# Retention and mixture of experts on one core: zero products in the first gaps, masks made on the chip, and routing steps written later in the program

## The chip, the cores and the metric

The kernel runs on one core of a Trainium2 chip. TensorE (PE in the rows) multiplies, with weight loads shown as PEld; VectorE is DVE, ScalarE is ACT, GpSimd is POOL, and SyncE is SP, which here issues nearly all loads. The metric is device microseconds for one execution of the whole program; less is better.

## The reference

```python
for t in range(S):                                   # B=4, H=8, S=768, D=64
    state = gamma * state + einsum('bhd,bhe->bhde', k[:, :, t], v[:, :, t])
    y[:, :, t] = scale * einsum('bhd,bhde->bhe', q[:, :, t], state)
x = y.transpose(0, 2, 1, 3).reshape(3072, 512)
logits = x @ w_gate + modality_bias[modality_id]     # 8 experts
e_idx = argmax(logits); gate_w = softmax(logits) at e_idx
out[mask_e] = gate_w * (relu(x[mask_e] @ w1[e]) @ w2[e])   # w1 512x1024, w2 1024x512
```

So: a retention (linear attention with a decay per head) over 3072 tokens, then each token goes through the one expert of the eight that its logits choose.

## The kernel before, in words

**Retention.** The 3072 tokens are 24 chunks of 128, six to a batch row. For chunk n PE makes the scores `sc` (line 174), whose product with a triangular mask DVE writes to `abuf` (line 179); the products `y` of the query with the state `s` of the chunk before (line 198) and of `abuf` with the decayed values `vd` (line 210); the state `st` (line 246), which ACT copies to `s` (line 251); and the tokens `x` (line 227), which are `yT` times a matrix of an identity and the gate weights, and which ACT copies to `xs` (line 231). DVE makes `yT` out of `y` (line 217) and sums the logits `lg` (line 232); POOL makes `vd` (line 162); ACT makes the table `dq` (line 156). Chunks 0 and 1 run singly (`one_chunk`), the others in pairs (`two_chunks`); in the pair n, n+1 the scores are those of chunks n+2 and n+3 and the tokens those of n-2 and n-1.

**Routing.** After every six chunks the group of six is routed. `route_a` finds the expert (parts 0 and 1) and the gate value (part 2: `den`, `rec`); `route_b` counts ranks on PE (`rk`, lines 369 and 370); `route_c` turns them into row numbers (`rkt`, `pos`). `scatter` then has POOL write the group's chunks, one by one, to `xsl`, a buffer in device memory sorted by expert (line 391). There are nine `xs` tiles, so the copy of chunk 9 into its tile first waits until the scatter of chunk 0 has landed.

**Experts.** Jobs of 512 slots each run behind the retention: two early ones (`e0`, `e1`), placed when twelve chunks are routed, and four at the end (`f0` to `f3`). A job loads its rows (`rows_in`: `xb`), transposes them on DVE (line 710), splits them into a high and a low part (ACT line 716, DVE line 725: `xT`), does the same with its weights (`raw`, `cut`), and multiplies (line 733: `h`; line 751: `o`), 32 steps of six products each. The results are scaled by the gate (lines 763 to 766) and scattered to the output by POOL (line 767).

**What sets the order.** PE, ACT, DVE and SP take their instructions in the order in which the program writes them. The pairs have named places ("top", "st", "sc", "pr", "tk", "end"), and `at(n, place, f)` hangs a routing or job step on the place of chunk n. All small PE results share eight banks of PSUM through the one tag "bank"; a tile waits until the bank's last reader is through. `warm` multiplies zeros, with no use for the result, before the first scores and after them.

Of the kernel before, what the change touches and what calls it, by code (L numbers as in the profile page):

```python
# [46 lines left out]
WARM = (10, 4)  # L47
# [8 lines left out]
def kernel(  # L56
# [199 lines left out]
    def warm(i):  # L256

        z = abuf[:, 3, 0, : DM // 2]
        if i == 0:
            nc.vector.memset(z, 0.0)  # L260
        z = z.bitcast(BF16)
        w = bank("warm")
        for _ in range(WARM[i]):
            nc.tensor.matmul(w, z[:, :P], z, start=True, stop=True)

    gates = cp.tile([P, NG, NE], F32, name="gates")

# [476 lines left out]
    def second(s, hh, part):  # L746
# [9 lines left out]
        if part == 3:  # L756
# [4 lines left out]
            if s is jobs[-1] and hh == HH - 1:  # L761
                h = DM // 2
                nc.vector.tensor_scalar(o[:, h:], s.po[:, h:], gate, None, op0=ALU.mult)
                nc.scalar.activation(o[:, :h], s.po[:, :h], AF.Copy, scale=gate)
            else:
                nc.scalar.activation(o, s.po, AF.Copy, scale=gate)  # L766
# [127 lines left out]
    for g in range(NGRP - 1):  # L894
# [3 lines left out]
        at(t + 2, "st", route_b, g)  # L898
        early = g + 1 in EARLY
        if early:  # L900
            at(t + 2, "st", early_a, g + 1)
        at(t + 2, "st", route_c, g)
        at(t + 2, "st", route_a, g, 2)
# [11 lines left out]
        places = [(2, "end"), (3, "sc"), (4, "sc"), (4, "end"), (6, "sc"), (6, "end")]  # L915
        if early or t + 6 == NN:
            places[2:] = [(4, "sc"), (4, "end"), (5, "sc"), (5, "end")]
# [6 lines left out]
    at(t + 3, "sc", two, raw, e, 1, (2, 3))  # L924
    at(t + 6, "top", rows_in, e)
    at(t + 6, "sc", cut, e, 1, 0, True)
    at(t + 6, "end", raw, e, 2, 0)
    n = t + 8
    at(n, "sc", flip_t, e, 0)
    at(n, "sc", flip_hi, e, 0)  # L930
    at(n, "tk", flip_lo, e, 0)
# [10 lines left out]
    def loads(n):  # L942

        for i in (n, n + 1):
            if i < NN:
                load_kq(i)
        for i in (n, n + 1):
            if i < NN:
                load_kv(i)

# [43 lines left out]
    def one_chunk(n):  # L994
# [3 lines left out]
        state(n)  # L998
        decay_q(n)
# [9 lines left out]
        heads_a(n)  # L1009
        run(n, "end")  # L1010
# [10 lines left out]
    def last_tokens():  # L1021
        g = NGRP - 1
        tokens_out(NN - 1)
        assert not hooks, hooks
        yield
# [86 lines left out]
    with tc.manual_schedule(engines={PE, ACT, DVE, SP}):  # L1112
        load_kq(0, True)
        nc.scalar.dma_start(cst, consts[:, :C_BIG])
        nc.scalar.dma_start(csq, consts[:, C_BIG:])
# [3 lines left out]
        nc.sync.dma_start(dcq, decq)  # L1119
        load_kv(1)  # L1120
        for n in range(SINGLE, LEAD, 2):
            loads(n)
# [9 lines left out]
        warm(0)  # L1132
        scores(0)
# [6 lines left out]
        tokens_out(NN - 2)  # L1140
# [28 lines left out]
def _layout(inputs):  # L1169
# [14 lines left out]
    cst = np.zeros((P, C_BIG + C_END), f)  # L1184
# [81 lines left out]
```

## Time and profile before

| | |
|---|---|
| time, median of 3 runs | 391.02 us (390.77 to 391.48) |
| the profiled execution's own time | 388.42 us |
| its span, first to last instruction | 386.6 us |
| TensorE busy | 374.3 us, 97% |
| VectorE, ScalarE, GpSimd busy | 203.7, 156.1, 100.6 us |
| HBM read and written | 65.05 and 23.41 MB |

The profiled execution is 2.6 us shorter than the median; sums are made on the profiled one and carried over as a difference. A row of the timeline gives start, duration, engine, line, operation, out<-in, count, and in brackets how long the engine stood idle and what released it. A busy PE may still be waiting inside a group of products; such a wait shows as a longer group.

### The profile page before, as it was taken

To read this page: it belongs to the slowest core of one execution; us is meant where nothing else is said; L and a number is where in the kernel's file an instruction comes from. 1 tells how busy PE (TensorE), PEld (TensorE's weight loads), DVE (VectorE), ACT (ScalarE), POOL (GpSimd) and SP (SyncE) were. 2 spreads that over 40 slices of the span, in tenths; PEclk is the share of its full clock that TensorE was granted. 3 is DMA by queue.
4 is the path that set the end of the run, shared out by engine and by line. 5 is a ranking of instruction groups with operands and counts; after the bars stand their busy time and mean duration, and the time that the engine had idled before them with its cause. 6 is when DMAs were issued, how large, how long until landed. Compare 5 with 4: busy or idle time off the path is not lost. (4 is left out here: it accounts for less than half of the span.)

```text
span 386.6 us, 7963 instructions
## 1 busy us (share of the span) xinstructions
PE 374.3 (97%) x2977; PEld 311.1 (80%) x2977; DVE 203.7 (53%) x418; ACT 156.1 (40%) x303; POOL 100.6 (26%) x141
## 2 busy tenths in 40 slices
PE   8999999999899999999999999999999999999993
PEld 4799888987787788888877888778888888888882
DVE  1876858868668982448243382433832466144100
ACT  1455535553665262345423453224532344244110
POOL 1342474664810887100210102101021002100121
PEclk9999999999999999999999999999999999999998
DMA  7999899999449659497973878738343674400001
GB/s 266 390 376 391 345 332 382 317 412 200 162 125 231 242 200 323 173 191 267 326 278 98 182 249 316 280 112 165 108 163 110 160 166 152 148 28 3 27 27 52
DMA packets 40474, 81.94 MB, mean 212 GB/s; under 512 B 8173, under 2 KB 20589, under 8 KB 40177
## 3 DMA queue, kind: packets, MB, share of 16 engines
q1 hardware_dynamic: 34720, 65.72, 54.1%
q0 software_dynamic: 5136, 15.21, 10.1%
q8 instruction: 25, 0.41, 0.4%
q10 hardware_dynamic: 576, 0.46, 0.4%
q14 instruction: 17, 0.14, 0.1%
HBM read 65.05 MB, written 23.41 MB: 229 GB/s over the span
## 5 line engine op out<-in xcount | busy, mean ns | idle before, releaser
L733 PE MATMUL h_f<-xT_f,hi_f 128*128 128x512 f32 x256 | 81.1, 392 | 0.0
L751 PE MATMUL o_f<-hi_f,hT_f 128*128 128x512 f32 x256 | 78.8, 389 | 0.0
L696 DVE TENSOR_TENSOR lo_f<-raw_f,hi_f 128x1024 fp32r<-128x1024 f32 x32 | 39.2, 1226 | 34.0 <-ACT hi_f L691 33.8
L733 PEld LDWEIGHTS h_f<-xT_f,hi_f 128*128 128x128 f32 x256 | 48.1, 188 | 11.1 <-issue 1.2
L751 PEld LDWEIGHTS o_f<-hi_f,hT_f 128*128 128x128 f32 x256 | 48.1, 188 | 10.0
L741 DVE SCALAR_TENSOR_TENSOR hT_f<-h_f,hT_f 128x512 fp32r<-128x512 f32 x32 | 22.2, 693 | 63.2 <-ACT hT_f L740 63.2
L733 PE MATMUL h_f<-xT_f,lo_f 128*128 128x512 f32 x128 | 49.9, 390 | 0.0
L751 PE MATMUL o_f<-lo_f,hT_f 128*128 128x512 f32 x128 | 49.8, 389 | 0.0
L767 POOL DMA_INDIRECT out_dram<-o_f,tg_f x16 | 15.7, 982 | 127.1 <-ACT o_f L766 112.3
L740 ACT ACTIVATE hT_f<-h_f 128x512 fp32r<-128x512 f32 x32 | 19.2, 599 | 54.4 <-PE h_f L733 54.4
L733 PE MATMUL h_e<-xT_e,hi_e 128*128 128x512 f32 x128 | 40.6, 393 | 0.0
L751 PE MATMUL o_e<-hi_e,hT_e 128*128 128x512 f32 x128 | 39.5, 390 | 0.0
L179 DVE TENSOR_TENSOR abuf<-sc,csq 128x512 f32<-128x512 f32 x48 | 30.1, 680 | 13.8 <-PE sc L174 7.1
L691 ACT CAST hi_f<-raw_f 128x1024 fp32r<-128x1024 f32 x32 | 33.3, 1041 | 0.0
L162 POOL TENSOR_TENSOR vd<-kv,cst 128x512 f32<-128x512 f32 x24 | 24.9, 1044 | 31.7 <-DMA kv<-in_qkv_dram 16.6
L751 PEld LDWEIGHTS o_f<-lo_f,hT_f 128*128 128x128 f32 x128 | 24.0, 188 | 5.0
L733 PEld LDWEIGHTS h_e<-xT_e,hi_e 128*128 128x128 f32 x128 | 24.0, 188 | 4.9
L751 PEld LDWEIGHTS o_e<-hi_e,hT_e 128*128 128x128 f32 x128 | 23.9, 188 | 4.9
L733 PEld LDWEIGHTS h_f<-xT_f,lo_f 128*128 128x128 f32 x128 | 24.0, 188 | 4.8
L766 ACT ACTIVATE o_f<-o_f,tg_f 128x512 f32<-128x512 f32 x15 | 10.3, 689 | 42.7 <-PE o_f L751 42.7
L174 PE MATMUL sc<-kq 64*128 64x128 f32 x384 | 27.0, 282 | 0.5 <-DMA kq<-in_qkv_dram 0.3
L391 POOL DMA_INDIRECT xsl<-xs,pos x24 | 25.4, 1059 | 7.7 <-POOL xs L387 5.3
(168 smaller groups left out, 526.3 us busy)
## 6 DMA issues: line engine op xcount, KB each, us to landing
raw_f<-in_w_dram SPq DMA_DIRECT2D x32, 512.0 KB, 3.5
kq<-in_qkv_dram SPq DMA_DIRECT2D x23, 512.0 KB, 7.0
kv<-in_qkv_dram SPq DMA_DIRECT2D x19, 512.0 KB, 9.1
raw_e<-in_w_dram SPq DMA_DIRECT2D x16, 512.0 KB, 4.3
xb_f<-xsl SPq DMA_DIRECT2D x16, 256.0 KB, 5.8
abuf<-in_w_dram SPq DMA_DIRECT2D x8, 512.0 KB, 4.8
rw<-in_w_dram SPq DMA_DIRECT2D x16, 256.0 KB, 6.8
xb_e<-xsl SPq DMA_DIRECT2D x8, 256.0 KB, 6.0
```

The source lines that it names most:

```text
L162: nc.gpsimd.tensor_tensor(vds[n], vv, dec[:, n % NCH].unsqueeze(2).to_broadcast([P, H, D]), op=ALU.mult)
L174: nc.tensor.matmul(pe[j][:, g * P : (g + 1) * P], kt[r, g], qt[r, g], start=True, stop=True, skip_group_check=True,)
L179: nc.vector.tensor_tensor(a[:, j], pe[j].rearrange("p (h t) -> p h t", t=P), mask.unsqueeze(1).to_broadcast([P, NG, P]), op=ALU.mult,)
L391: ins = nc.gpsimd.indirect_dma_start(out=xsl[:, :], out_offset=bass.IndirectOffsetOnAxis(ap=mid[gr][:, i : i + 1], axis=0), in_=xs.rearran ...
L691: nc.scalar.copy(hi, t)
L696: nc.vector.tensor_tensor(lo, t, hi.bitcast(F32), op=ALU.subtract)
L733: nc.tensor.matmul(s.ph, s.w[1][f // 2][wi][:, o : o + P], s.xT[kc][a], start=(kc == 0 and k == 0), stop=(kc == KC - 1 and k == 2),)
L740: nc.scalar.activation(hi, s.ph, AF.Relu)
L741: nc.vector.scalar_tensor_tensor(lo, s.ph, 0.0, hi.bitcast(F32), op0=ALU.max, op1=ALU.subtract)
L751: nc.tensor.matmul(s.po, s.hT[f][a][:, hh * P : (hh + 1) * P], s.w[2][f // 2][wi][:, (f % 2) * DM : (f % 2 + 1) * DM], start=(f == 0 and k ...
L766: nc.scalar.activation(o, s.po, AF.Copy, scale=gate)
L767: ins = nc.gpsimd.indirect_dma_start(out=out[:, :], out_offset=bass.IndirectOffsetOnAxis(ap=s.tg.bitcast(I32)[:, hh, 0:1], axis=0), in_=o, ...
```

## The change

It consists of these parts.

- `warm`: 12 instead of 10 zero products before the first scores, 4 after them as before, and new ones in chunk 0: 2 behind its state and 3 behind its `y`.
- The identity and the triangular mask (`csq`) are no longer loaded (128 KB on ACT's queue). POOL makes a ramp by an iota, and DVE compares it twice.
- The table `dcq` (256 KB), asked for ahead of the keys and values of chunk 1 before, is asked for behind the third load of keys and queries.
- In the groups that are not early, `route_b` moves from "st" to "tk" of the second pair, and `route_c` and the gate value to its "end"; the first two scatters move half a chunk or so.
- The first job's transposes (`flip_t`, `flip_hi`, `flip_lo` for its first quarter) move from "sc" and "tk" of chunk 20 to "top" and "sc" of chunk 21. Two of its weight loads move behind `rows_in`.
- The tokens of chunks 22 and 23 are written one step of the first job later.
- The last result is halved between DVE and ACT by partitions (64 x 512 each) instead of by columns (128 x 256 each), and the two are declared independent.

```diff
-WARM = (10, 4)
+WARM = (12, 4, 2, 3)
...
+    def setup_masks():
+        pin(
+            nc.gpsimd.iota(
+                ident, [[1, P]], base=0, channel_multiplier=-1,
+                allow_small_or_imprecise_dtypes=True,
+            )
+        )
+        nc.vector.tensor_scalar(mask, ident, 0.0, None, op0=ALU.is_ge)
+        nc.vector.tensor_scalar(ident, ident, 0.0, None, op0=ALU.is_equal)
...
-                h = DM // 2
-                nc.vector.tensor_scalar(o[:, h:], s.po[:, h:], gate, None, op0=ALU.mult)
-                nc.scalar.activation(o[:, :h], s.po[:, :h], AF.Copy, scale=gate)
+                a, b = slice(0, D), slice(D, P)
+                ins = nc.vector.tensor_scalar(o[a], s.po[a], gate[a], None, op0=ALU.mult)
+                disjoint(ins, "halves")
+                ins = nc.scalar.activation(o[b], s.po[b], AF.Copy, scale=gate[b])
+                disjoint(ins, "halves")
...
-        at(t + 2, "st", route_b, g)
         early = g + 1 in EARLY
+        at(t + 2, "st" if early else "tk", route_b, g)
...
-        at(t + 2, "st", route_c, g)
-        at(t + 2, "st", route_a, g, 2)
+        at(t + 2, "st" if early else "end", route_c, g)
+        at(t + 2, "st" if early else "end", route_a, g, 2)
...
-        places = [(2, "end"), (3, "sc"), (4, "sc"), (4, "end"), (6, "sc"), (6, "end")]
-        if early or t + 6 == NN:
-            places[2:] = [(4, "sc"), (4, "end"), (5, "sc"), (5, "end")]
+        places = [(3, "sc"), (3, "end"), (4, "sc"), (4, "end"), (6, "sc"), (6, "end")]
+        if t + 6 == NN:
+            places[4:] = [(5, "sc"), (5, "end")]
+        if early:
+            places = [(2, "end"), (3, "sc"), (4, "sc"), (4, "end"), (5, "sc"), (5, "end")]
...
-    at(t + 3, "sc", two, raw, e, 1, (2, 3))
     at(t + 6, "top", rows_in, e)
+    at(t + 6, "top", two, raw, e, 1, (2, 3))
...
-    at(n, "sc", flip_t, e, 0)
-    at(n, "sc", flip_hi, e, 0)
-    at(n, "tk", flip_lo, e, 0)
+    at(n + 1, "top", flip_t, e, 0)
+    at(n + 1, "top", flip_hi, e, 0)
+    at(n + 1, "sc", flip_lo, e, 0)
...
         state(n)
+        if n == 0:
+            warm(2)
...
         heads_a(n)
+        if n == 0:
+            warm(3)
...
         g = NGRP - 1
+        tokens_out(NN - 2)
+        yield
         tokens_out(NN - 1)
         assert not hooks, hooks
-        yield
         yield
...
-        nc.scalar.dma_start(cst, consts[:, :C_BIG])
-        nc.scalar.dma_start(csq, consts[:, C_BIG:])
+        nc.scalar.dma_start(cst, consts)
...
-        nc.sync.dma_start(dcq, decq)
```

**The order on DVE, around the scores of chunks 10 and 11.** These are DVE's instructions from `yT` of chunk 7 on, before and then in the change; the number behind a name is the program's own counter, and `abuf<-sc_10` is the masking of the scores of chunk 10.

```order
L217 TENSOR_TENSOR yT_710<-y_7_661,dq_587 128x256
L179 TENSOR_TENSOR abuf<-sc_10_738,csq 128x512
L179 TENSOR_TENSOR abuf<-sc_10_739,csq 128x512
L376 TENSOR_TENSOR rkt_753<-rk_750,oh_652 128x48
L379 TENSOR_REDUCE pos_755<-rkt_753 128x6
L361 TENSOR_REDUCE den_757<-ex_91 128x6
L363 RECIPROCAL rec_759<-den_757 128x6
L179 TENSOR_TENSOR abuf<-sc_11_761,csq 128x512
L179 TENSOR_TENSOR abuf<-sc_11_762,csq 128x512
L232 TENSOR_REDUCE lg_775<-xs_776 128x8
L232 TENSOR_REDUCE lg_775<-xs_786 128x8
```

```order
L217 TENSOR_TENSOR yT_721<-y_7_672,dq_598 128x256
L179 TENSOR_TENSOR abuf<-sc_10_749,csq 128x512
L179 TENSOR_TENSOR abuf<-sc_10_750,csq 128x512
L179 TENSOR_TENSOR abuf<-sc_11_761,csq 128x512
L179 TENSOR_TENSOR abuf<-sc_11_762,csq 128x512
L232 TENSOR_REDUCE lg_775<-xs_776 128x8
L232 TENSOR_REDUCE lg_775<-xs_789 128x8
L377 TENSOR_TENSOR rkt_804<-rk_786,oh_663 128x48
L380 TENSOR_REDUCE pos_806<-rkt_804 128x6
L362 TENSOR_REDUCE den_808<-ex_91 128x6
L364 RECIPROCAL rec_810<-den_808 128x6
```

The four routing instructions, of which `pos` and `rec` are what the scatters wait for, stand behind the masking of chunk 11 and the logits of chunks 6 and 7. At chunks 22 and 23 the same four move in the same way.

**The order on DVE, around chunks 22 and 23.** These rows follow the masking of chunk 22; `x_e` is the first job's first transpose, which needs the rows `xb_e`, and `xT_e<-x_e,xT_e` is its low part. ACT makes the high part (line 716) out of the same transpose; that cast stands, before, in front of ACT's four copies `xs` of chunks 18 and 19, and in the change behind them and behind the table `dq`.

```order
L376 TENSOR_TENSOR rkt_1665<-rk_1662,oh_1579 128x48
L379 TENSOR_REDUCE pos_1667<-rkt_1665 128x6
L361 TENSOR_REDUCE den_1669<-ex_91 128x6
L363 RECIPROCAL rec_1671<-den_1669 128x6
L179 TENSOR_TENSOR abuf<-sc_23_1673,csq 128x512
L179 TENSOR_TENSOR abuf<-sc_23_1674,csq 128x512
L710 STREAM_TRANSPOSE x_e_1687<-xb_e_1501 128x512
L232 TENSOR_REDUCE lg_1691<-xs_1692 128x8
L725 TENSOR_TENSOR xT_e_1689<-x_e_1687,xT_e_1689 128x512
L232 TENSOR_REDUCE lg_1691<-xs_1703 128x8
L217 TENSOR_TENSOR yT_1751<-y_20_1723,dq_1565 128x256
```

```order
L232 TENSOR_REDUCE lg_1687<-xs_1688 128x8
L232 TENSOR_REDUCE lg_1687<-xs_1701 128x8
L377 TENSOR_TENSOR rkt_1716<-rk_1698,oh_1590 128x48
L380 TENSOR_REDUCE pos_1718<-rkt_1716 128x6
L362 TENSOR_REDUCE den_1720<-ex_91 128x6
L364 RECIPROCAL rec_1722<-den_1720 128x6
L711 STREAM_TRANSPOSE x_e_1724<-xb_e_1508 128x512
L217 TENSOR_TENSOR yT_1756<-y_20_1728,dq_1576 128x256
L217 TENSOR_TENSOR yT_1756<-y_20_1729,dq_1576 128x256
L726 TENSOR_TENSOR xT_e_1726<-x_e_1724,xT_e_1726 128x512
```

The logits of chunks 18 and 19 no longer stand behind the transpose, and the low part stands behind `yT` of chunk 20. The transpose itself stays ahead of `yT` of chunk 20.

**The order on PE, where the first job begins.** The first row of each is the last of the retention's `y`; `x_0` and `x_1` are the two halves of a chunk's tokens, first those of chunk 22 and then those of chunk 23, and `h_e` are the first job's products.

```order
L210 MATMUL y_23_1838<-abuf,vd_1685 64x128 x4
L227 MATMUL x_0_1881<-wgt,yT_1855 128x136 x2
L227 MATMUL x_1_1885<-wgt,yT_1855 128x136 x2
L733 MATMUL h_e_1896<-xT_e_1689,hi_e_1541 128x512
L733 MATMUL h_e_1896<-xT_e_1689,lo_e_1543 128x512
L733 MATMUL h_e_1896<-xT_e_1689,hi_e_1541 128x512
L733 MATMUL h_e_1896<-xT_e_1781,hi_e_1541 128x512
L733 MATMUL h_e_1896<-xT_e_1781,lo_e_1543 128x512
L733 MATMUL h_e_1896<-xT_e_1781,hi_e_1541 128x512
L227 MATMUL x_0_1904<-wgt,yT_1872 128x136 x2
```

```order
L210 MATMUL y_23_1849<-abuf,vd_1685 64x128 x4
L734 MATMUL h_e_1897<-xT_e_1726,hi_e_1552 128x512
L734 MATMUL h_e_1897<-xT_e_1726,lo_e_1554 128x512
L734 MATMUL h_e_1897<-xT_e_1726,hi_e_1552 128x512
L734 MATMUL h_e_1897<-xT_e_1792,hi_e_1552 128x512
L734 MATMUL h_e_1897<-xT_e_1792,lo_e_1554 128x512
L734 MATMUL h_e_1897<-xT_e_1792,hi_e_1552 128x512
L227 MATMUL x_0_1905<-wgt,yT_1866 128x136 x2
L227 MATMUL x_1_1909<-wgt,yT_1866 128x136 x2
```

The job's first step of six products now stands ahead of the tokens of chunk 22, and its second step ahead of those of chunk 23.

## Rows read from the trace of the kernel before

**Rows 1.** The page's first part: busy time, share of the span, instructions.

```profile
PE 374.3 (97%) x2977; PEld 311.1 (80%) x2977; DVE 203.7 (53%) x418; ACT 156.1 (40%) x303; POOL 100.6 (26%) x141
```

**Rows 2.** Windows: stretch, length, busy of PE, PEld, DVE, ACT, POOL, clock, DMA, GB/s.

```profile
5.00:10.00 5.00, 4.68 (x60) 3.08 (x60) 1.47 (x3) 0.37 (x1) 1.04 (x1) 1.00 1.04 392
...
90.00:100.00 10.00, 8.08 (x118) 6.90 (x120) 7.70 (x23) 4.13 (x14) 4.59 (x10) 1.00 0.87 189
```

**Rows 3.** Timeline of the opening.

```profile
1.19 4.45 PE L264 MATMUL warm<-abuf 128*128 128x512 bf16 x10 [1.19 <-DVE abuf L260]
...
6.38 1.04 POOL L162 TENSOR_TENSOR vd<-kv,cst 128x512 f32<-128x512 f32 x1 [5.38 <-DMA cst<-in_consts_dram]
...
6.66 1.04 PE L264 MATMUL warm<-abuf 128*128 128x512 bf16 x4
...
7.85 1.29 DVE L179 TENSOR_TENSOR abuf<-sc,csq 128x512 f32<-128x512 f32 x2 [6.71 <-DMA csq<-in_consts_dram]
...
8.63 1.16 PE L174 MATMUL sc<-kq 64*128 64x128 f32 x16 [0.32 <-DMA kq<-in_qkv_dram]
...
10.63 1.04 POOL L162 TENSOR_TENSOR vd<-kv,cst 128x512 f32<-128x512 f32 x1 [3.21 <-DMA kv<-in_qkv_dram]
...
11.73 0.69 PE L246 MATMUL st<-vd,kv 128*64 128x64 f32 x16 [0.91 <-POOL vd L162]
```

**Rows 4.** Timeline around the first group's gate values and its first scatter.

```profile
44.66 0.19 DVE L363 RECIPROCAL rec<-den 128x6 f32<-128x6 f32 x1
44.77 1.25 DVE L179 TENSOR_TENSOR abuf<-sc,csq 128x512 f32<-128x512 f32 x2
...
45.93 0.32 DVE L232 TENSOR_REDUCE lg<-xs 128x8 f32<-128x32 f32 x2
46.02 1.18 POOL L391 DMA_INDIRECT xsl<-xs,pos  x1 [0.76 <-ACT xs L231]
...
55.33 0.67 ACT L231 COPY xs<-x 128x272 f32<-128x272 f32 x2 [2.86 <-DMA xsl<-xs,pos]
...
56.38 0.87 PE L246 MATMUL st<-vd,kv 128*64 128x64 f32 x16
```

**Rows 5.** DMA issued from 47.5 to 48.0: KB each, us to landing.

```profile
kv<-in_qkv_dram SPq DMA_DIRECT2D x1, 256.0 KB, 11.3
xsl<-xs,pos POOLq DMA_INDIRECT x1, 8.9
```

**Rows 6.** Timeline from the scores of chunk 23 to the first job.

```profile
91.95 1.49 PE L174 MATMUL sc<-kq 64*128 64x128 f32 x16
...
96.67 0.71 DVE L710 STREAM_TRANSPOSE x_e<-xb_e 128x512 f32<-128x512 f32 x1 [0.67 <-DMA xb_e<-xsl]
...
97.42 0.62 ACT L716 CAST xT_e<-x_e 128x512 fp32r<-128x512 f32 x1 [5.12 <-DVE x_e L710]
97.94 1.24 ACT L231 COPY xs<-x 128x272 f32<-128x272 f32 x4
...
98.38 0.66 PE L198 MATMUL y<-kq,s 64*64 64x128 f32 x14 [1.88 <-ACT xs L231]
...
98.77 0.69 DVE L725 TENSOR_TENSOR xT_e<-x_e,xT_e 128x512 fp32r<-128x512 f32 x1
...
101.01 0.86 DVE L217 TENSOR_TENSOR yT<-y,dq 128x256 f32<-128x256 f32 x2 [0.48 <-PE y L210]
...
104.42 1.97 PE L210 MATMUL y<-abuf,vd 128*64 128x128 f32 x32
...
107.03 1.16 PE L227 MATMUL x<-wgt,yT 128*128 128x136 f32 x8 [0.65 <-DVE yT L217]
...
109.43 1.09 PE L227 MATMUL x<-wgt,yT 128*128 128x136 f32 x8
```

**Rows 7.** Timeline of the last result.

```profile
380.17 0.48 DVE L763 TENSOR_SCALAR o_f<-o_f,tg_f 128x256 f32<-128x256 f32 x1 [20.37 <-PE o_f L751]
380.69 0.47 ACT L764 ACTIVATE o_f<-o_f,tg_f 128x256 f32<-128x256 f32 x1 [5.27 <-DVE o_f L763]
```

More of the change, by code (lines that the diff above doesn't have):

```diff
@@ L254, in small @@
         return cp.tile(shape, dt, name=nm)
[L256 to L264, printed above, removed]
-    gates = cp.tile([P, NG, NE], F32, name="gates")
+    gates = cp.tile([P, NG, NE], F32, name="gates")
+    def setup_masks():
[7 more added lines that the diff above has]
+        nc.vector.tensor_scalar(ident, ident, 0.0, None, op0=ALU.is_equal)
     def setup_a():
@@ L940, with loads @@
     at(n + 3, "sc", flip_lo, e, 3)
-    def loads(n):
+    def loads(n, tab=None):
         for i in (n, n + 1):
@@ L946, in loads @@
                 load_kq(i)
+                if tab is not None and i == n:
+                    nc.sync.dma_start(tab, decq)
         for i in (n, n + 1):
@@ L949, in loads, with warm @@
                 load_kv(i)
+    def warm(i):
+        z = abuf[:, 3, 0, : DM // 2]
+        if i == 0:
+            nc.vector.memset(z, 0.0)
+        z = z.bitcast(BF16)
+        w = bank("warm")
+        for _ in range(WARM[i]):
+            nc.tensor.matmul(w, z[:, :P], z, start=True, stop=True)
     def two_chunks(n):
@@ L1118 @@
         load_kq(1)
-        nc.sync.dma_start(dcq, decq)
         load_kv(1)
         for n in range(SINGLE, LEAD, 2):
-            loads(n)
+            loads(n, dcq if n == SINGLE else None)
             if n == SINGLE + 2:
@@ L1132 @@
         warm(0)
+        setup_masks()
         scores(0)
@@ L1139 @@
             two_chunks(n)
-        tokens_out(NN - 2)
         r = last_tokens()
@@ L1183, in _layout @@
     t = np.arange(S, dtype=np.float64) + 1.0
-    cst = np.zeros((P, C_BIG + C_END), f)
-    cst[:, C_BIG + C_ID : C_BIG + C_ID + P] = np.eye(P)
-    cst[:, C_BIG + C_MASK :] = np.triu(np.ones((P, P)))
+    cst = np.zeros((P, C_BIG), f)
     dec = (gam[None, :] ** (-t[:, None])).reshape(NCH, P, H)
```

## Prediction

> **What bounds the kernel now.** I read the page's first part first. TensorE is busy 97% of the span and the next engine, VectorE, 53% [rows 1]. So no other engine's saving counts by itself; what counts is where TensorE stands still, and what is added to or taken from its own list. The windows come next: one stretch of the opening and the ten microseconds around the end of the retention [rows 2]. In the latter TensorE is busy for only 8.08 of 10.00 us, at full granted clock, so that is where something is to be had. The timelines then say what it waited for. In the opening it waits 0.32 us for keys and queries ahead of the second chunk's scores, and 0.91 us ahead of the second state for POOL's `vd`, which itself waited for `kv` [rows 3]. At chunk 20 it waits 1.88 us inside the `y` products for ACT's copies `xs`, and 0.65 us ahead of chunk 22's tokens for `yT` [rows 6]. The last result is scaled in two steps after TensorE is through [rows 7]. Everything between stands on TensorE's own list: a microsecond saved or lost there moves the end by a microsecond.
>
> **The change part by part.** *The first job and the last tokens.* ACT works in order. Its cast of `x_e` waited 5.12 us for the transpose on DVE, which waited for the job's rows, and the four copies `xs` stood behind that cast; TensorE needed the bank those copies free [rows 6]. In the change the cast stands behind the copies and behind `dq`. Nothing that TensorE needs is then behind the transpose on ACT, so the 1.88 us go: −1.88. The rank products `rk` leave the stretch between the scores of chunks 22 and 23. Scores of 16 products took 1.49 us there against 1.16 us in the opening [rows 3, 6], and I put the difference down to the bank that `rk` held: −0.33. Third, chunk 22's tokens now stand behind the job's first step of six products. Before, heads ended at 106.39 (104.42 + 1.97) and TensorE waited until 107.03; tokens and step took 2.40 us a chunk (109.43 − 107.03), so both chunks' pairs ended at 111.83 [rows 6]. After, heads end 2.2 us earlier, at 104.2, and the first step (2.40 less the tokens' 1.09, so 1.3) lasts to 105.5. DVE must have finished chunk 22's `yT` by then. Its list from the `yT` of chunk 21, moved up by the same 2.2 us (from 101.01 to 98.8, 0.86 long), is: three transposes of 0.71, two or three low parts of 0.69, some logits of about 0.2, with ACT's casts of 0.62 between, and `yT` itself [rows 6]; laid end to end with the casts that hold it up it reaches 105.65. So a wait of some 0.15 us is left of the 0.65, and tokens, step and tokens (1.1 + 1.3 + 1.1) end at 109.15, against 111.83: −2.7, with rounding −2.8 for the whole part, of which about 0.6 is the third piece. Bounds: −1.6 if only the wait on ACT goes and 0.3 of it comes back at `yT`, −3.4 if the last tokens wait for nothing at all. Two weight loads of 512 KB now go behind `rows_in` on SP's queue; the stretch moves 189 GB/s, while the opening moved 392 [rows 2], so they are late for nothing before the second half of the weights is cut, tens of steps later; cost nothing, and if that cover were gone 1 MB at 392 GB/s is 2.7 us.
>
> *The first group's routing.* Here the change adds a wait. `rkt`, `pos`, `den` and `rec` go behind the masking of chunk 11 and two logits. Before, `rec` ended at 44.85, POOL had its two small instructions done soon after, and the first scatter was issued at 46.02, having waited for `xs` [rows 4]. After, the logits still wait for those same copies and end at about 46.25 less the little that the masking gains; four instructions of 0.19 follow, then POOL's two small ones of 0.4 in all: 47.2 to 47.5, so 1.2 to 1.5 us later. Behind it on POOL stand the second scatter and a `vd`. The scatter needed 9.3 us (46.02 to 55.33), and its landing ended a wait of 2.86 us on ACT ahead of chunk 9's copy; behind that copy (0.67) on ACT stands the copy of the state, and TensorE's next state product at 56.38 needs both [rows 4]. TensorE has no idle time there, so its slack is unknown: nothing is lost if the scatter lands sooner relative to its issue, 1.5 if not. I take the middle, +0.8 (0 to +1.5). That `rk` leaves this pair gains nothing: the masking, 1.25 us for each chunk, is DVE's chain there and not TensorE's [rows 4].
>
> *The opening.* Ten zero products took 4.45 us, the four later ones 1.04 us, so 0.44 and 0.26 each, which is the lower and the upper level (1.2 and 2.4 GHz) of the clock; the window from 5 us on has 1.00 granted [rows 2, 3]. Seven are new: two in front, 0.5 to 0.9 together, and five in the gaps, 1.3. In all 1.8 to 2.2 us are added to TensorE's list. Their cover is the 0.32 and the 0.91 us [rows 3], and these shrink too: `csq` and `dcq`, 393 KB, no longer stand ahead of `kv` of chunk 1, at 392 GB/s [rows 2] 1.0 us, so `vd` of chunk 1 is there at 10.7 instead of 11.67. TensorE's list without waits would bring it to the second state at 10.5; with two plus two zero products ahead (the three others partly behind it), at 11.6 to 11.9, against 11.73. So +0.2 (−0.4 to +0.8). The masks are new on POOL and DVE and no row has either. Before, the masking started at 7.85, when `csq` had landed. POOL's `vd` of chunk 0 ends at 7.42 [rows 3]; the ramp behind it and two compares on DVE lie between almost nothing and, priced as a `vd` (1.04) and two maskings (0.64 each), 9.7. By size, a quarter of the elements of either, I expect 8.3. The first reader on TensorE is `y` of chunk 0, not before 9.4 or so; so nothing, or +0.4 at worst. The table `dcq` is read by the first `yT` at about 11, with over 2 us to spare.
>
> *The last result.* ACT's half ended its wait on DVE's: 380.17 + 0.48, then 0.47 [rows 7]. Side by side with 64 x 512 each, a half costs between 0.48 and twice that; I take 0.75 against 0.99: −0.25 (−0.5 to +0.5, the latter if they still go one after the other).
>
> The other moved scatters belong to groups whose tiles are not waited for in the rows: nothing. Sum: −2.8 + 0.8 + 0.2 − 0.25 = −2.05 against the profiled 388.42, that is 386.4. The median of the runs is 2.6 us above the profiled one, and I carry the difference over: 391.02 − 2.05 = 389.0. The forecast's own range is 387.7 to 390.2.
>
> **The rivals.** *The scatter decides; slower.* SP's load issued next to the second scatter took 11.3 us to land, that scatter 8.9 [rows 5]. If the first scatter, issued 1.4 us later, queues behind the loads that SP issues meanwhile, it lands at up to 58.9 instead of 55.3 (47.6 + 11.3), and TensorE loses up to 3.7 instead of 0.8: −2.05 + 2.9 = +0.85, 391.9. From 2.85 us of delay on nothing is left of the gain; slower by the bound from 3.6 on. For it speaks that ACT already waits there, against it that a scatter issued beside the load took 2.4 us less. The Trainium skill, in "DMA: Bandwidth & Descriptors", section "Queues, rings and completion order", has each transfer engine go round-robin between queues, packet by packet, which speaks against first come, first served; the two landings agree with it.
>
> *The rows come late; same.* DVE's transpose of `x_e` still stands ahead of `yT` of chunk 20. It ended at 97.38, and `yT` will be wanted at about 98.8, so 1.4 us are free. Each microsecond later than that stops DVE and then TensorE; rows 3 us later cost 1.6, 390.6, and so `same`. Before, the rows ended DVE's wait of 0.67 [rows 6], which speaks for it; two loads fewer ahead of them speak against it.
>
> *The zero products are not covered.* If waits in the opening don't shrink, all 1.9 us are on the path instead of 0.2: −2.05 + 1.7 = −0.35, 390.7, same.
>
> *The clock.* The profiled opening is at the upper level from about 5 us. If the timed runs are not, and this is the 2.6 us between them and the profiled one, zero products in the gaps could keep the level up: up to −2.6 more, 386.4. The Trainium skill, in "TensorE: Matmul & The Clock Gate", Part 1, says that the low clock is the default and activity releases it, and that the moment varies from run to run; no row here shows an opening that stays low.
>
> **How the numbers follow.** The forecast has 0.60, slower by the scatter 0.11, late rows 0.13, uncovered zero products 0.10, the clock 0.06. A difference within 0.2%, 0.78 us, is about what a measurement of this kernel can't tell from no change. The forecast's range lies almost wholly on the faster side (390.2 is its edge); with the clock and a small part of the others 0.68 is faster; the late rows, the uncovered products and half of the scatter's cases make 0.21 same; 0.11 is left for slower. The range of 80% takes the forecast's whole range, and reaches up to the rivals that end at same and down to −3.7, halfway to the clock's: 387.3 to 391.2.
>
> **What would show it.** After the change the timeline should have: no wait of TensorE for `xs` at chunk 20's `y`, and the first job's step ahead of chunk 22's tokens with less than 0.3 us of wait; scores of chunk 23 at about 1.16; the first scatter issued 1.2 to 1.5 later and the wait of ACT ahead of chunk 9's copy about as long, with TensorE's wait behind it of 0 to 1.5; the second state at 11.6 to 11.9 and the first masking not after 8.5; DVE's and ACT's last halves overlapping. The prediction is wrong if TensorE waits 2.85 us or more around chunk 9, if `y` of chunk 20 or 21 waits for DVE behind the transpose, or if waits in the opening stay as they were.

## Result and the profile of the changed kernel

| | before | change |
|---|---|---|
| median of the timed runs | 390.94 us (390.77 to 391.48, 4 runs) | 386.93 us (386.40 to 387.30, 4 runs) |
| the profiled execution | 388.42 us, span 386.6 | 386.61 us, span 384.8 |

The ratio is 0.9894 (0.9877 to 0.9911): 4.0 us faster, where 2.05 were forecast, and just under the range. But from profile to profile it is only 1.81 us. So there are two questions: whether the 1.81 us are made up as forecast, and where the other 2.2 us of the timed runs come from.

**The opening** of the change (timeline), against [rows 3]:

```profile
1.19 4.28 PE L967 MATMUL warm<-abuf 128*128 128x512 bf16 x12 [1.19 <-DVE abuf L963]
...
7.60 0.24 POOL L263 IOTA csq<- 128x128 f32 x1
...
8.13 0.23 DVE L269 TENSOR_SCALAR csq<-csq 128x128 f32<-128x128 f32 x1
8.28 1.28 DVE L179 TENSOR_TENSOR abuf<-sc,csq 128x512 f32<-128x512 f32 x2
...
9.91 1.04 POOL L162 TENSOR_TENSOR vd<-kv,cst 128x512 f32<-128x512 f32 x1 [2.07 <-DMA kv<-in_qkv_dram]
...
10.97 0.82 PE L967 MATMUL warm<-abuf 128*128 128x512 bf16 x3
11.72 0.69 PE L246 MATMUL st<-vd,kv 128*64 128x64 f32 x16
```

The masks cost 0.24 and twice 0.23 us, and the masking starts at 8.28 (8.3 expected). `vd` of chunk 1 starts 0.72 us earlier. The second state starts at 11.72 against 11.73, so what the new zero products take is about what the earlier masks and values give.

**The first group's routing** (timeline), against [rows 4]:

```profile
46.23 0.19 DVE L364 RECIPROCAL rec<-den 128x6 f32<-128x6 f32 x1
...
47.59 1.18 POOL L392 DMA_INDIRECT xsl<-xs,pos  x1 [0.75 <-POOL xs L388]
...
55.92 0.68 ACT L231 COPY xs<-x 128x272 f32<-128x272 f32 x2 [3.92 <-PE y L210]
56.48 0.39 ACT L251 COPY s<-st 128x256 f32<-128x256 f32 x1
56.97 0.69 PE L246 MATMUL st<-vd,kv 128*64 128x64 f32 x16 [0.45 <-issue]
```

The first scatter is issued 1.57 us later. ACT's copy of chunk 9, which waits for its landing, starts 0.59 us later (55.92 against 55.33). The bracket names PE's `y`, the last event of an engine; in the two other profiles of the change the same copy has `<-DMA xsl<-xs,pos` (3.86 and 3.89 us). Behind it on ACT stands the copy of the state, here from 56.48 and before from 55.89:

```profile
55.89 0.39 ACT L251 COPY s<-st 128x256 f32<-128x256 f32 x1
```

The state product starts 0.10 us behind the end of this copy in both (56.97 and 56.38). It is chunk 13's, written behind the `y` of chunk 11.

**The first job** (timeline), against [rows 6]:

```profile
92.07 2.51 PE L174 MATMUL sc<-kq 64*128 64x128 f32 x32
...
96.69 1.10 PE L198 MATMUL y<-kq,s 64*64 64x128 f32 x32
...
99.04 0.62 ACT L717 CAST xT_e<-x_e 128x512 fp32r<-128x512 f32 x1 [0.68 <-DVE x_e L711]
...
103.18 1.97 PE L210 MATMUL y<-abuf,vd 128*64 128x128 f32 x32
...
105.08 0.50 PE L734 MATMUL h_e<-xT_e,hi_e 128*128 128x512 f32 x1
...
105.84 0.75 DVE L217 TENSOR_TENSOR yT<-y,dq 128x256 f32<-128x256 f32 x2
...
106.57 1.09 PE L227 MATMUL x<-wgt,yT 128*128 128x136 f32 x8
...
108.88 1.09 PE L227 MATMUL x<-wgt,yT 128*128 128x136 f32 x8
```

The wait for `xs` is gone, 32 products of `y` run through in 1.10 us, and the tokens of chunk 22 stand behind the job's step without a wait.

**The last result** (timeline), against [rows 7]:

```profile
378.26 0.68 ACT L767 ACTIVATE o_f<-o_f,tg_f 64x512 f32<-64x512 f32 x1 [4.75 <-PE o_f L752]
378.26 0.74 DVE L765 TENSOR_SCALAR o_f<-o_f,tg_f 64x512 f32<-64x512 f32 x1 [20.38 <-PE o_f L752]
379.77 0.98 POOL L771 DMA_INDIRECT out_dram<-o_f,tg_f  x1 [5.00 <-DVEq L1170]
```

The halves do run side by side (0.74 us against 0.99), but POOL's scatter stands 0.77 us behind them, where it stood 0.28 behind the later half before (381.16 to 381.44). From the first scaling to the end of the span it is 6.54 us, against 6.43 before.

### The profile page after: what moved, and what is told of

Read it like the earlier page. It is cut to its first block, busy times and chain, and to the rows that moved or that the text cites. A ratio compares the mean times of both kernels' runs of the same rounds, so it can differ in the third digit from the quotient of the medians.

```text
span 384.8 us, 7973 instructions
## 1 busy us (share of the span) xinstructions
PE 374.3 (97%) x2983; PEld 311.2 (81%) x2984; DVE 203.8 (53%) x420; ACT 156.8 (41%) x303; POOL 101.0 (26%) x142
## 4 chain that ended last, share of the span: by engine, by line
PE 92%; DVE 2%; issue 2%; DMA 1%; POOL 0%; ACT 0%; POOLq 0%; ACTq 0%
PE h_f L734 23%; PE o_f L752 22%; PE h_e L734 11%; PE o_e L752 11%; PE x L227 6%; PE sc L174 6%; PE y L210 5%; PE y L198 3%; PE st L246 2%; DMA cst<-in_consts_dram 1%; PE ro L858 1%; PE rh L836 1%; DVE cum L356 1%; DVE oh L347 1%; PE warm L967 0%
## 5 line engine op out<-in xcount | busy, mean ns | idle before, releaser
L392 POOL DMA_INDIRECT xsl<-xs,pos x24 | 24.6, 1026 | 7.7 <-POOL xs L388 5.5
```

The costliest lines, as they stand in the source:

```text
L392: ins = nc.gpsimd.indirect_dma_start(out=xsl[:, :], out_offset=bass.IndirectOffsetOnAxis(ap=mid[gr][:, i : i + 1], axis=0), in_=xs.rearran ...
```

## Experiments

The runs were made on four later occasions, each on another chip and each with its own runs of the kernel before; medians are compared within an occasion. The expectations carry letters for the causes that the 2.6 us between profile and timed runs might have: A, the clock in the opening; B, transfers or the fetching of instructions; C, something outside the change that differs from occasion to occasion; D, the clock that falls in the middle because TensorE stands still in a wait; R, the rival of D.

### The kernel before again, and one part at a time

The first four runs share 7 runs of before, median 388.30 us.

**The kernel before, unchanged.**

> The kernel before, once more, with its own profile and with the span and granted clock of each run. Theory A (the opening's clock): the profiled execution of before (388.42 us) ran its opening at the upper level from 5 us on, and its timed runs (390.8 to 391.5) did not; then the runs fall into two groups, near 388.4 and near 391, and a profile of one near 391 shows zero products or the first scores at the lower level for longer than the 4.45 us that ten zero products took, with a granted clock under 1.00 in the windows up to 10 us, and nothing else longer. Theory B (the 2.6 us lie elsewhere, in transfers or in fetching instructions): a profile near 391 has the same opening and its 2.6 us in stretches behind 20 us. Ratio to before 1.000 by both.

Median 388.47 (387.99 to 388.82), ratio 0.9996 (0.9968 to 1.0025). No run of it is near 391; of the seven shared runs of before one is (390.57), and it has the lowest mean granted clock, 0.992; the others have 0.995 to 0.999. In its profile the ten zero products take 4.35 us and the first scores 1.16, as at 388.42. So this profile tells nothing of a long run; what is new is that the kernel before takes 388.3 on this occasion, not 391, which is C's forecast.

**Zero products alone.**

```diff
-WARM = (10, 4)
+WARM = (12, 4, 2, 3)
```

(with the two places in chunk 0 of the change)

> The kernel before with the zero products of the change alone (12, 4, 2, 3 in place of 10, 4). Theory A: the timed runs come down by about 2.0 us to 388.8 to 389.4, since the upper level then comes early in all of them; less what the seven products cost, up to 0.5. Theory B: the seven products cost 0.2 to 1.9 us and give nothing, 391.1 to 392.9.

388.37, ratio 0.9996 (0.9966 to 1.0025): in the kernel before they neither cost nor give. That does not show what they take of TensorE, since the wait at chunk 20 takes up part of what is won or lost ahead of it: in three profiles of the unaltered kernel the product behind that wait starts at 98.38, 98.34 and 98.35 us, with waits of 1.88, 1.21 and 1.12.

**The change without new zero products.**

```diff
-WARM = (12, 4, 2, 3)
+WARM = (10, 4)
```

> The change with the zero products of before (10, 4, none in the gaps). Theory A: the timed runs go up from 386.9 by about 2 us to 388.5 to 389.5, while a run whose opening is at the upper level anyway is at 386.4 to 386.6. Theory B: 386.4 to 386.9, no slower than the change, or faster by the product time that is not covered.

385.86 (385.33 to 387.40), not slower; the opening's clock loses nothing without them. Its timeline has the second state at 11.16, 0.56 us earlier than in the change; 0.36 of this is gone by the state product of chunk 2 (15.88 against 16.07). At the state product of chunk 13

```profile
55.73 0.67 ACT L231 COPY xs<-x 128x272 f32<-128x272 f32 x2 [3.93 <-PE y L210]
56.29 0.39 ACT L251 COPY s<-st 128x256 f32<-128x256 f32 x1
...
56.78 0.91 PE L246 MATMUL st<-vd,kv 128*64 128x64 f32 x16 [1.08 <-POOL vd L162]
```

0.19 us is left. The first scatter was issued 0.19 earlier too (47.40), and the product again starts 0.10 behind the end of ACT's copy of the state. The bracket names POOL's `vd` because that was the last event seen; the `vd` then running, from 55.33, belongs to a later chunk, and this product does not read it.

**The change with the first group's routing as before.**

```diff
-        at(t + 2, "st" if early else "tk", route_b, g)
+        at(t + 2, "st" if early or g == 0 else "tk", route_b, g)
...
+        if g == 0:
+            places[:2] = [(2, "end"), (3, "sc")]
```

(`route_c` and the gate value likewise)

> The change with the routing steps and the first two scatters of the first group alone at their places of before. The profiles have TensorE 0.47 us ahead of before at chunk 8 and 0.59 us behind it at the state product of chunk 11 (56.97 against 56.38), so 1.06 us went in between. If that is the later first scatter: 385.6 to 386.2, 0.7 to 1.1 us less than the change, and the state product at about 55.9. If it is something else, such as the order of the loads: within 0.3 us of the change.

385.52 (385.06 to 387.10). The second state is at 11.69 as in the change, and the state product of chunk 13 has no wait in brackets:

```profile
56.63 0.69 PE L246 MATMUL st<-vd,kv 128*64 128x64 f32 x16
```

That is 0.34 us before the change's, not the 1.06 expected. The first scatter is issued 1.43 us earlier than in the change (46.16), but ACT's copy of chunk 9, which waits for it, starts only 0.34 earlier (55.58), and the product goes by that copy.

### Change, first job's part, and openings

The next four runs share 29 runs of before, median 389.06 us (387.19 to 391.21).

**The change again.**

> The change once more. Profile against profile it is 1.8 us shorter than before; the first comparison of timed runs gave 4.0. Theory C (the timed runs of before were 2.6 us longer there than the kernel takes on other occasions, for a reason outside the change): where before takes 388.3, the change takes 386.2 to 386.8, 1.5 to 2.1 less. Theory A (the opening's clock, which the new zero products keep up): the difference depends on the opening; where runs of before have an early rise of the clock it is 1.8, and runs of before near 390.6 have counterparts of the change that stay at 386.5.

387.10 (385.92 to 387.94, 12 runs), ratio 0.9951 (0.9929 to 0.9972): 1.96 us less, inside C's 1.5 to 2.1. Of the 29 runs of before, seven have a mean clock of 0.993 or less; they have a median of 390.26, the other 22 one of 388.70. None of the change's twelve has such a clock. Against the 22 the change still gains 1.60.

**Fewer zero products in the kernel before.**

```diff
-WARM = (10, 4)
+WARM = (4, 4)
```

> The kernel before with 4 zero products ahead of the first scores in place of 10. In the profiles the upper level comes 3.2 to 4.3 us after the first product; TensorE now stands still from about 2.9 us until the first keys land, so the level should rise later, by 1.5 to 3 us. Theory A: the scores, state and y of the first chunks at the lower level take twice as long, and the end moves by 1 to 2.6 us, to 389.3 to 390.9. If the wait for keys, masks and kv covers it all: within 0.4 us of before.

389.09, ratio 1.0001 (0.9976 to 1.0025): an opening with the second state 0.68 us later (12.41) does not move the median. This ends theory A, though the wait at chunk 20 may hide a smaller loss. But the profiled execution was a long one (391.28, mean clock 0.993), and its timeline and its windows (length, TensorE busy, granted clock, DMA share, GB/s) show where:

```profile
99.39 0.66 PE L198 MATMUL y<-kq,s 64*64 64x128 f32 x14 [1.95 <-ACT xs L231]
99.98 1.45 PE L210 MATMUL y<-abuf,vd 128*64 128x128 f32 x16
...
102.06 1.93 PE L210 MATMUL y<-abuf,vd 128*64 128x128 f32 x16
103.92 2.14 PE L227 MATMUL x<-wgt,yT 128*128 128x136 f32 x16
```

```profile
99.00:100.00 1.00, 0.61 (x16) 1.00 0.17 65
100.00:101.00 1.00, 1.00 (x18) 0.79 0.53 213
101.00:102.00 1.00, 1.00 (x21) 0.50 0.19 60
102.00:103.00 1.00, 1.00 (x16) 0.50 0.63 231
103.00:104.00 1.00, 1.00 (x11) 0.51 0.53 213
104.00:105.00 1.00, 1.00 (x9) 1.00 0.18 70
```

Behind the wait at chunk 20 the granted clock goes from 1.00 to 0.50, the lower level, and comes back at 104. From `y` to the tokens it takes 3.94 us (99.98 to 103.92). The profile of before at 388.42 took 2.36 (98.97 to 101.33), with the clock at 1.00. The loss is 1.58 us; the missing clock of the windows, 1.70 us of 389, lowers the mean by 0.0044, about the step from most other runs (0.994 to 0.999) to 0.992 or 0.993. In every profile the granted clock falls once more behind TensorE's last product, 1.6 to 4.5 us before the end of the span, where it costs nothing; this tail is why the mean of a run without a fall also varies, and why 0.993 is only a rough mark. A fall behind the wait, because TensorE stands still there, is theory D.

**The first job's part alone**, on the kernel before.

```diff
-    at(t + 3, "sc", two, raw, e, 1, (2, 3))
     at(t + 6, "top", rows_in, e)
+    at(t + 6, "top", two, raw, e, 1, (2, 3))
...
-    at(n, "sc", flip_t, e, 0)
+    at(n + 1, "top", flip_t, e, 0)
...
+        tokens_out(NN - 2)
+        yield
         tokens_out(NN - 1)
```

> The kernel before with the first job's transposes, its two weight loads and the last tokens moved as in the change, and nothing else of it (the rank products of the last pair stay between its scores). By my terms: 1.88 for ACT's wait and 0.6 for the last tokens, so 2.5 us less than before; in the profiles before waits only 1.2 us there on this occasion, so 1.7 to 2.5. If the gain needs the moved routing of the last pair: under 1 us.

386.36 (385.35 to 387.25, 10 runs), ratio 0.9936 (0.9913 to 0.9959): 2.70 us less than before, and 0.74 less than the whole change on the same occasion. This part is more than all of the gain. That the others cost 0.74 together, where my terms for them add up to 0.75, is partly luck: the runs of the two kernels overlap, and piece by piece the profiles differ from the terms (below). None of its ten runs has a clock of 0.993 or less.

**The change with the first group's routing and the zero products of before.** The two edits above together.

> The change with the first group's routing and first two scatters at their places of before and with the zero products of before. Each alone gave 0.5 to 1.1 us against the change's profile: the state product of chunk 11 without the wait for POOL's vd (1.06 us), the second state at 11.16 instead of 11.72 (0.56 us). If both add: 1.2 to 1.6 us less than the change, about 385.0 where the change takes 386.5. If the 0.56 us are lost again to vd or to keys behind it: 385.5.

385.22 (384.73 to 386.06, 6 runs), 1.88 us less than the change on the same occasion, where 1.2 to 1.6 were expected if both add. The state product of chunk 13 stands at 55.76, 1.21 us before the change's:

```profile
55.76 0.94 PE L246 MATMUL st<-vd,kv 128*64 128x64 f32 x16
```

The first scatter is issued at 45.45 here, and ACT's copy of chunk 9 starts at 54.71, 1.21 us before the change's. So the zero products were covered in part only: the second state is at 11.47 to 11.76 in the five profiles of the change and its variants with the new ones, and at 10.51 to 11.16 in the three without. By the state product of chunk 2 it is, against before, −0.26 to +0.20 us with them and −0.62 to −0.20 without.

### Does standing still let the clock fall?

Four runs with 29 runs of before, median 389.45 us (387.73 to 392.16); seven of the 29 at 0.993 or less, their median 390.76 against 388.94.

**Zero products in the wait at chunk 20.**

```diff
+        if n == NN - 4:
+            y = pys[n][0].rearrange("p c t -> p (c t)")
+            for _ in range(10):
+                nc.tensor.matmul(
+                    y, zero[:, :P], zero, start=False, stop=False, skip_group_check=True
+                )
         heads_s(n + 1)
```

> The kernel before, with ten zero products of 128x256 written behind the first y of chunk 20, ahead of the product that waits for ACT's copies; they add zeros to a result that is not complete yet, so nothing is left out. The wait for xs stays; TensorE multiplies zeros for about 1.1 us of it. Theory D (new: the profile of the kernel with fewer zero products shows the granted clock at 0.50 from 101 to 104 us, behind the 1.95 us wait at chunk 20; those of before at 388.4 do not, and in 29 runs of before all of 389.9 and more with a mean clock of 0.993 or less): no run with that clock any more, none over 389.5, median 387.8 to 388.3, that is 0.8 to 1.2 under before, at no shorter wait. Rival R (the clock falls for another reason, or the long runs have another cause): the same spread as before, 387.2 to 391.2, and a median not under that of before.

389.36 (388.29 to 391.20), ratio 1.0003 (0.9983 to 1.0024). A miss for D: no run was to have the low clock, and two of twelve have 0.991 and 0.992 (390.77, 391.20); the median has not moved. In the profile, ten products fill the wait (1.26 us) without a rest; that they leave a longer wait open in the two low runs is a guess, since neither has a profile. The profiled run itself (389.90) is long without a fall. ACT's cast of the first weights waits 2.81 us there for their landing, and the copies that TensorE needs stand behind it:

```profile
86.93 1.04 ACT L693 CAST hi_e<-raw_e 128x1024 fp32r<-128x1024 f32 x1 [2.81 <-DMA raw_e<-in_w_dram]
...
88.31 1.09 PE L210 MATMUL y<-abuf,vd 128*64 128x128 f32 x16 [1.07 <-ACT xs L231]
```

That cast's wait is 0.75 to 2.81 us in the profiles of this study (0.77 in that of before, 0.75 in that of the change), and between 81.7 and 90.0 us TensorE loses up to 2.0 us against the profile of before. It may be a second cause of long runs, next to the clock; no run was made for it.

**A longer wait.** ACT makes its cast of the first transpose three times.

```diff
-        nc.scalar.copy(t[:, 0], s.x[kc])
+        for _ in range(3 if s is jobs[0] and kc == 0 else 1):
+            nc.scalar.copy(t[:, 0], s.x[kc])
```

> The kernel before with ACT's cast of the first transpose made three times, which holds back the copies xs of chunks 18 and 19, and so the wait at chunk 20, by 1.24 us more. Theory D: the clock falls behind it in nearly every run; 1.24 for the wait and 1.6 for the clock (3.3 us at 0.50) on the runs without a fall (388.0): 390.8 or more in nearly all, mean clock 0.993 or less. Rival R: 1.24 us more on each run of before, 388.5 to 392.4, a third of them at the low mean clock as before.

391.65 (389.52 to 394.34), 2.2 us over before for 1.24 us of wait; eight of twelve runs at 0.993 or less, against seven of 29. The windows of its profile (394.34, wait 2.42) have the fall too, at a mean clock of 0.994:

```profile
104.00:105.00 1.00, 1.00 (x22) 0.63 0.69 238
105.00:106.00 1.00, 1.00 (x18) 0.50 0.15 48
106.00:107.00 1.00, 1.00 (x13) 0.50 0.69 274
107.00:108.00 1.00, 1.00 (x9) 0.67 0.51 191
```

**The longer wait, filled** (another occasion, with 21 runs of before, median 390.06; eight at 0.993 or less). The wait of the last run, and 20 zero products in it.

> The kernel before with the wait at chunk 20 lengthened by 1.24 us, as in the run with the longer wait, and with 20 zero products, some 2.2 us, written into it. Theory D (the clock falls because TensorE stands still): the falls go, mean clock 0.994 or more in nearly all runs, and 389.8 to 390.6 where the longer wait alone took 391.65 and had 9 of 12 runs at 0.992 or less. Rival R (it falls for what comes late, not for TensorE's standing still): the same low clock in most runs, 391.4 or more.

390.16 (388.85 to 392.77), ratio to before 1.0012 (0.9984 to 1.0040); one of twelve runs at 0.993, the others at 0.995 or more, where the same wait unfilled had eight at 0.993 or less. Its windows:

```profile
100.00:101.00 1.00, 0.86 (x11) 1.00 0.18 65
101.00:102.00 1.00, 1.00 (x22) 1.00 0.62 248
102.00:103.00 1.00, 1.00 (x30) 1.00 0.54 200
```

From the tokens to the `y` with `abuf` it takes 6.14 us in both profiles (95.41 to 101.55 here, 97.33 to 103.47 unfilled), so the wait is as long, and the clock stays. So, by these counts, what makes the clock fall is TensorE's standing still and not what comes late. This is theory D's forecast; the two counts (eight, where the expectation says nine, and one) were taken on different occasions.

**The change without the first job's part.** The first job's part above, taken back.

> The change with the first job's transposes, its two weight loads and the last tokens at their places of before: the wait of TensorE for ACT's copies at chunk 20 is back. By the sum of the profiles 1.9 to 2.5 us more than the change, 389.0 to 389.6 where the change takes 387.1. Theory D: in some runs 1.6 us more on top, with a mean clock of 0.993 or less, so that the runs spread over 388 to 391 as those of before do, though all other parts of the change are in. Rival R: the narrow spread of the change, 2 us.

389.67 (388.14 to 391.08), ratio to before 1.0015 (0.9994 to 1.0036): without this part the change gives nothing. The wait at chunk 20 is back and can take up what the other parts cost or give. But none of twelve runs is at 0.993 or less, a miss for D: in its profile the wait is 1.22 us, which is no shorter than in most profiles of before, and yet 23 of 86 runs of before have the low clock. Why none has it here is not shown.

**The kernel before, two single runs.**

> The kernel before, one look. Theory D: if it takes 389.9 or more with a mean clock of 0.993 or less, the granted clock is at 0.50 for about 3 us behind the wait at chunk 20, and this wait is longer than the 1.9 us of the profile at 388.4; if it takes 388.9 or less, no fall. Rival R: a long run shows no such stretch.

> The kernel before, a second look, as in the first look: a long run with a low mean clock has its fall behind the wait at chunk 20 (theory D), or has none there (rival R).

388.52 (clock 0.998) and 388.83 (0.995): both short, both with a wait of 1.12 us at chunk 20 and no fall. They fit D, but there is no profile of the unaltered kernel before with a fall.

**The change a third time**, beside the filled wait.

> The change a third time. Theory D: no run of it with a mean clock of 0.993 or less, 1.5 to 2.5 us less than before in the median, more on an occasion on which more runs of before have the low clock. If 4.0 is the change's own: 3.5 to 4.5.

386.47 (385.53 to 387.33, 10 runs), ratio 0.9922 (0.9893 to 0.9950): 3.6 us less. By then eight of the 21 runs of before were at 0.993 or less (median 390.83); against the other 13 (389.12) the change gains 2.65.

### A last result in one instruction

The kernel with the first group's routing and the zero products of before, with the last result scaled by ACT alone:

```diff
-                a, b = slice(0, D), slice(D, P)
-                ins = nc.vector.tensor_scalar(o[a], s.po[a], gate[a], None, op0=ALU.mult)
-                ins = nc.scalar.activation(o[b], s.po[b], AF.Copy, scale=gate[b])
+            nc.scalar.activation(o, s.po, AF.Copy, scale=gate)
```

> The kernel with the first group's routing and the zero products as before and the rest of the change, and the last result scaled by ACT alone in one instruction of 128x512. The halves side by side took 0.74 us, and POOL's scatter came 0.77 us behind their end; the other results, scaled by ACT alone in 0.69 us, had their scatter 0.27 us behind it. So 1.51 becomes 0.96: about 0.5 us less, 384.6 to 384.8 where the kernel with halves takes 385.2. If the 0.77 us belongs to the last result and not to the two engines: the same or 0.05 less.

```profile
376.78 0.69 ACT L762 ACTIVATE o_f<-o_f,tg_f 128x512 f32<-128x512 f32 x1 [4.75 <-PE o_f L752]
377.74 0.98 POOL L763 DMA_INDIRECT out_dram<-o_f,tg_f  x1 [4.45 <-ACTq L1160]
```

384.67 us (384.48 to 386.55), ratio to before 0.9893 (0.9865 to 0.9920), on the occasion whose runs of before have 389.45. The scatter comes 0.27 us behind the one instruction, 0.96 behind the start instead of 1.51; the span is 0.5 us shorter than with halves (382.9 against 383.4). It is the quickest kernel of this study; it and the change were not run on one occasion, but against each occasion's runs of before it gains 4.8 us, and the change 4.0, 2.0 and 3.6.

## Why the prediction was wrong

**The step that failed** is "I carry the difference over: 391.02 − 2.05 = 389.0". The 2.6 us between the profiled execution of before and its timed runs are not a constant that the change keeps: the change's timed runs are 0.3 us over its profiled one. The median of before was 390.94, 388.30, 389.06, 389.45 and 390.06 us on five occasions, that of the change 386.93, 387.10 and 386.47 on three. So the change takes away most of what makes before vary.

Part of that is the clock. A wait that is removed was priced by its length in one execution; in others it also costs the clock. 23 of the 86 runs of before on the four later occasions had a mean clock of 0.993 or less and were 1.6 to 2.3 us longer than the others in the median; of the 56 runs of kernels without the wait none had. The rest is not explained. Against the runs of before without the low clock the change still gained 1.60 us on one occasion and 2.65 on another, and ten of the 31 runs of before at 390.0 or more have a clock of 0.994 or more; the landing of the first weights may be one cause of those, but none of them has a profile. The four runs of before in the first comparison, 390.77 to 391.48, lie where most runs have a fall (seven of the eight later ones between the same bounds), but their clocks are not known, and at a share of 23 in 86 four out of four would be unlikely by chance. Why that occasion was so slow stays open, and so does whether the chips differ.

The sum came out close, 386.4 forecast for the profiled execution and 386.61 measured, and that is partly luck: its terms were off by +0.3 (first group), −0.2 (`rk`), −0.2 (opening), −0.7 (first job) and +0.35 us (last result), and about 0.9 us was lost that no term has.

**The clock rival** had the number (386.4) and the wrong place: it looked for the clock in the opening. In every profile with ten or twelve zero products ahead of the first scores, TensorE is at the upper level by the end of those scores, 7.4 us at the latest; more products alone and fewer alone left the median of the kernel before where it was.

**First job and last tokens, −2.8:** right in mechanism, too small by 0.7. Two more rows of the timeline of before:

```profile
90.59 1.16 PE L174 MATMUL sc<-kq 64*128 64x128 f32 x16
...
93.37 2.12 PE L227 MATMUL x<-wgt,yT 128*128 128x136 f32 x16
```

From the scores of chunk 22 to the start of chunk 23's tokens it took 18.84 us before (90.59 to 109.43, [rows 6]) and, with one job step more, 16.81 after (92.07 to 108.88). That step took 1.49 (105.08 to 106.57), where the prediction had 1.3, so −3.5 in all, just outside its bounds. The wait of 1.88 was longer than its bracket: the 18 products ahead of it took 1.08 us where 32 take 1.10 after the change, so another half microsecond of waiting lies inside that group. The pair's scores, now without `rk` between them, take 2.44 us (92.07 to the first tokens at 94.51) against 2.78, as forecast. `yT` of chunk 22 ended 1.44 us behind the heads' end, as laid out (1.45), and the 0.65 went whole.

**The first group, +0.8:** it cost 1.06 us in the change's profile, inside the bounds of 0 to +1.5, and by the path forecast: scatter, copy of chunk 9, copy of the state, state product. From one state product to the next it takes 2.58 us (54.39 to 56.97) against 1.52 before (54.86 to 56.38). From the scatter's issue to the copy it takes 8.33 us in the change and 9.31 before, so the scatter does land sooner relative to its issue: 1.57 us later at the issue became 0.59 at the copy. In the five profiles whose scatter is moved it takes 8.0 to 8.3 us; at the old place it takes 9.2 to 9.5 in all but one, which has 8.2. Why is not shown. That `rk` leaves this pair I had put at nothing; from the scores of chunk 10 to the pair's first product with `abuf` it takes 5.82 us (40.21 to 46.03) against 6.06 (40.44 to 46.50), so it gave 0.24.

**The opening, +0.2:** 0.0. The second state came at the same time, and so did the state product of chunk 2 (16.07 against 16.08); the 0.23 us by which the change is ahead at the scores of chunk 10 come in between. **The last result, −0.25:** +0.1. The halves took the 0.75 us expected; POOL's scatter stood 0.77 us behind the two of them instead of 0.28 and ate it.

**Not forecast:** in the change's profile TensorE lost about 0.9 us around chunk 16, at a state product, with no releaser named (0.24 and 0.38 in brackets):

```profile
81.41 0.37 PE L246 MATMUL st<-vd,kv 128*64 128x64 f32 x5 [0.24 <-issue]
82.17 0.26 PE L246 MATMUL st<-vd,kv 128*64 128x64 f32 x1 [0.38 <-issue]
```

The two other profiles of the change lack this stop, but lose 0.9 and 0.6 us a little later, where ACT's cast waits longer for the first weights (1.72 and 1.39 us). What stopped the first one stays open, as does why the first group's old place together with the old zero products gave 1.88 us in the medians where the spans differ by 0.9 to 1.4.

**The rivals.** No rows came late: the transpose of `x_e` did not hold `yT` of chunk 20. The scatter's landing did decide the state product, but at 0.59 us and not at the rival's bound: it did not queue behind the loads for the 11.3 us of that rival. The zero products were covered in part: what they took was about what the earlier masks and values gave.

## What to carry to other kernels

Before a profile's time is carried over to a median, look at the spread of the runs and at each run's mean granted clock: a difference between the profiled execution and the rest can itself be the cost of a wait, and go with it. A wait of about 2 us of a TensorE that is otherwise full cost its own length here plus, in some runs, the clock behind it; where a long wait was filled with zero products, the second was saved though the first stayed. A mean clock also contains the tail behind the last product, so a single run near the mark tells little.

What is won or lost ahead of a wait can vanish in it: a part that moves nothing in the kernel before can cost something once the wait is gone.

The name in a bracket is the last event seen, not always the releaser. Read in the program which tile the instruction needs, and look in several profiles for a fixed distance: here the state product started 0.10 us behind ACT's copy of the state wherever it waited.

## What the runs showed of the hardware

- The granted clock fell to 0.50 for about 3.4 us behind waits of 1.95 and 2.42 us at chunk 20, and not behind waits of 1.12, 1.21, 1.22 and 1.88 us there. A longer wait was followed by the low mean clock in eight of twelve runs, and the same wait filled with zero products in one of twelve. The Trainium skill, in "TensorE: Matmul & The Clock Gate", Part 1, says that the low clock is the default and that activity releases it. The filled wait agrees. Nothing here tells how the chip decides.
- In the openings the granted clock reads 1.00 while zero products of 128x512 start every 0.43 us, twice what they take later; there the level is read from the products, not from that column.
- POOL's scatter of the last result was issued 0.27 us behind one engine's end, 0.28 behind two halves that ended one after the other, and 0.77 behind two that ended together. Why is not shown.
